# Attention with a parallel MLP on one core: weighted sums in bursts of three key tiles, two in three steps

## The chip, the core and the metric

The kernel runs on one core of a Trainium2 chip. The metric is the time of one execution on the device in microseconds (us); the time of a kernel is the median of its runs. The engines have short names: PE (TensorE) multiplies matrices, PEld is its loading of stationary weights, DVE (VectorE), ACT (ScalarE) and POOL (GpSimd) work element by element, and SP only issues DMAs. Each engine carries out its own instructions in the order in which the kernel issues them, and waits where an operand is not ready or a buffer is not free. Results of PE land in PSUM, eight banks of 128 partitions by 512 f32 numbers; DVE and ACT read them from there.

## The reference

x has 2048 tokens of 448 numbers. One layer norm feeds two branches, and their sum is added to x:

```python
x = A_x
xn = _layernorm(x, axis=-1)
return x + _A_ref(xn, A_wq, A_wk, A_wv, A_wo) + _B_ref(xn, B_w1, B_b1, B_w2, B_b2)
```

Branch A is attention with 16 query heads of width 28 that share one head of keys and one of values:

```python
scores = jnp.einsum("bhqd,bkd->bhqk", q, k) * (Dh ** -0.5)
p = _softmax(scores, axis=-1)
o = jnp.einsum("bhqk,bkd->bhqd", p, v)
return (lambda x, *d: x.transpose(*d))(o, 0, 2, 1, 3).reshape(B, S, H * Dh) @ wo
```

Branch B normalizes once more, goes up to 1792 numbers with a GELU, and back to 448.

## The kernel before

The work has two phases. The first one (up to about 480 us) computes q, k, v and the MLP. The second one is the loop over `steps` at lines 871 to 912, and only this loop and what it calls is touched.

Queries are cut into 4 chunks of 512 and heads into 4 groups of 4, which gives 16 units (c, g); unit u is `units[u]`. Keys are cut into 16 key tiles of 128. A step is two key tiles of one unit, so a unit is 8 steps and the loop has 128 steps, numbered n from 0. The softmax needs the largest score of each query first, so scores are computed twice: once with queries on the partitions for the maximum, and once with keys on the partitions for the exponentials.

In units 1 to 15 (`TURNED`) the last of the four heads goes another way. Its scores are computed once, with queries on the partitions; the maximum and the exponential are taken there; the result goes to DRAM (`td`), and comes back in blocks (`half`) that DVE transposes. The three other heads, and all four of unit 0, are scored twice.

What a step does, and in which order, is a string of letters in `ORDERS`. There is one set of strings for unit 0 and one for the others, and the strings of a set are taken in turn by the number of the step. The letters are:

- `s`: one score tile of 128 keys by 512 queries (`score`, line 852). PE writes one PSUM bank (line 860), ACT takes the exponential of it into half of a weight buffer `p` (line 861).
- `m`: one tile for the maximum (`max_stream`, line 507). PE writes a bank (517), DVE reduces it (518). Its quota follows `weight` (line 875): an `m` is left out where the stream is ahead.
- `t`: one tile of the turned head (`turned_scores`, 545). PE writes a bank (551), DVE copies it with its maximum into one of two `raw` buffers (552). Four of them fill a `raw` buffer.
- `x`: half of the exponential of a full `raw` (`turned_exp`, 564; ACT, line 569). After the second half SP stores `raw` in four DMAs (572). A `raw` buffer can be written again when its store has read it.
- `T`: DVE transposes the turned head's blocks of this step's two key tiles (`turn_blocks`, 841) into one weight buffer.
- `P`: a burst of weighted sums, `BURST` key tiles long (`pv`, 824). For each key tile four heads run side by side in four strips of 32 columns of PE, two instructions each, so a burst of two key tiles is 16 instructions (line 829). They add into `po`, the eighth bank.
- `n`, `o`: one piece of the normalization of the unit before (`norm_jobs`, 754), and of the output projection (`o_jobs`, 734). `e`: the transposed maxima of the next unit, at one step of each unit (`load_max`, 493).

At the start of a step `load_d` (706) has DVE write one number into a `half` buffer and SP load into it (line 712 is that memset). A `half` buffer is a quarter-by-quarter filled block of eight key tiles, and there are three.

Tiles for `s`, `m`, `t`, `e` and `o` share a ring of seven PSUM banks (line 700):

```python
mp = ctx.enter_context(tc.tile_pool(name="ring", bufs=7, space=PSUM))
```

PE can start such a tile only when one of these banks has been read. The weight buffers `p` hold two tiles of 128 by 512, and there are `PAIRS` of them; a step of a turned unit takes four. `P` at step n reads the key tiles in order, behind the scores, and its buffers are free again after it. The last 11 steps (`LEAD`) have no `m`.

Of the kernel before, what the change touches and what calls it, by code (L numbers as in the profile page):

```python
# [8 lines left out]
F32 = mybir.dt.float32  # L9
F32R = mybir.dt.float32r  # L10
# [5 lines left out]
P = 128  # L16
S, D, H, DH, F = 2048, 448, 16, 28, 1792
NT = S // P
CT = 4
NCH = NT // CT  # L20
CW = CT * P
NG = H // 4
NF = F // P
EPS = 1e-5
SCALE = DH ** -0.5
BURST = 2
PAIRS = 9
MLP_MAX = 18
ORDERS = (("nsmsmsnomssmstmssxmP", "nsmsmsemssmsomssnxmP"), ("nmsstTmsosnmssP", "nmsmssxmeosTmsnsmP"))
TURNED = tuple(range(1, 16))  # L30
RAWS = 2
GELU = 0.044715, 0.7978845608028654
LEAD = 11
# [5 lines left out]
def block_kernel(ctx, tc, x, wq, wk, wv, wo, w1, b1, w2, b2, out):  # L39
# [4 lines left out]
    def f(t):  # L44
        return t.bitcast(F32)
# [8 lines left out]
    def heads_of(u):  # L54
        return 3 if u in TURNED else 4
# [56 lines left out]
    def mtile(shape):  # L112
        return mp.tile(shape, F32, name="m")
# [97 lines left out]
    def bn_end(c, k0=0, n=CT):  # L211
        for k in range(k0, k0 + n):
            dve.bn_aggr(lnp[:, CT * c + k, :], sts[c][:, k, :])
        ts = slice(CT * c + k0, CT * c + k0 + n)
        r = rstd(lnr[:, ts], lnp[:, ts, 1], n)
        next(r)
        yield
        next(r)
        dve.scalar_tensor_tensor(lnb[:, ts], lnp[:, ts, 0], -1.0, lnr[:, ts], op0=ALU.mult, op1=ALU.mult)
        yield  # L220
# [9 lines left out]
    def norm_both():  # L230
        dve.tensor_mul(lnq, lnp[:, :, 1], lnr)
        dve.tensor_mul(lnq, lnq, lnr)
        r = rstd(lnq, lnq, NT)
        next(r)
        yield
        next(r)
        dve.tensor_mul(lnq, lnq, lnr)
        dve.scalar_tensor_tensor(lnqb, lnp[:, :, 0], -1.0, lnq, op0=ALU.mult, op1=ALU.mult)
        act.activation(warm, one, AF.Tanh)
        yield  # L240
# [61 lines left out]
    def norm_gen(c, bank):  # L302
        center, turn = norm_parts(c, True, False, bank)
        for k in range(CT + 1):
            if k > 0:
                turn(k - 1)
            yield
            if k < CT:
                center(k)
            yield  # L310
# [83 lines left out]
    def spin(n, t=None):  # L394
        for _ in range(n):
            pe.matmul(idle if t is None else t, ident, ident, start=True, stop=True)
# [9 lines left out]
    for c, at in ((2, ((0, 1), (0, 2), (0, 2), (0, 3))), (3, ((1, 0), (1, 1), (1, 2), (1, 3)))):  # L406
        for k in range(CT):
            later(*at[k], lambda t=CT * c + k: bn(t))
        g = bn_end(c)
        for k in range(2):  # L410
            later(c - 1, 0, lambda g=g: next(g), True)
    g = norm_both()
# [13 lines left out]
    qss, ots = {}, {}  # L426
# [15 lines left out]
    for c in range(NCH):  # L442
        center, turn = norm_parts((c + 1) % NCH, c + 1 == NCH)
        for i in range(4):
# [7 lines left out]
            if i in ((2, 3) if c == 0 else (1, 3)):  # L452
                n = 2 * c + i // 3
# [209 lines left out]
    for c in range(1, NCH):  # L663
        g = norm_gen(c, lambda shape: php.tile(shape, F32, name="ph"))
# [4 lines left out]
    for n in range(len(mslots) + 2):  # L669
        c, ft = mslots[n] if n < len(mslots) else (NCH, n - len(mslots))  # L670
# [28 lines left out]
    att = ctx.enter_context(tc.tile_pool(name="att", bufs=2))  # L699
    mp = ctx.enter_context(tc.tile_pool(name="ring", bufs=7, space=PSUM))  # L700
    op = ctx.enter_context(tc.tile_pool(name="op", bufs=1, space=PSUM))

    wor = att.tile([P, NG, D], F32, name="wor", bufs=1)
    halves = {}

    def load_d(u, i):
# [5 lines left out]
        dve.memset(part[0:1, 0, 0:1], 0.0)  # L712
        nc.sync.dma_start(part, td[u][:, r, :, 256 * h:256 * h + 256])

    woh = att.tile([P, NG, D], F32R, name="woh", bufs=1)
    wol = att.tile([P, NG, D], F32R, name="wol", bufs=1)
    pool.memset(wor, 0.0)
# [10 lines left out]
    def load_rows_of(c, tiles):  # L728
        for k in tiles:
            rows[c, k] = keep.tile([P, D], F32, name="a", bufs=4)  # L730
            dve.memset(rows[c, k][0:1, 0:1], 0.0)
            nc.sync.dma_start(rows[c, k], ad[:, CT * c + k, :])

    def o_jobs(c, gs, tiles=range(CT)):
        last = NG - 1 in gs
        for k in tiles:
            po = mtile([P, D])
            ts = slice(k * P, (k + 1) * P)
            for g in gs:
                oth, otl = ots[c, g]  # L740
                pe.matmul(po, oth[:, ts], woh[:, g, :], start=(g == gs[0]), stop=False)  # L741
                pe.matmul(po, oth[:, ts], wol[:, g, :], start=False, stop=False)  # L742
                pe.matmul(po, otl[:, ts], woh[:, g, :], start=False, stop=(g == gs[-1]))  # L743
            a = rows[c, k]
            dve.tensor_add(a, a, po)
            if last:
                (nc.scalar if k % 2 and c == NCH - 1 else nc.sync).dma_start(ov[:, CT * c + k, :], a)
            yield

    def o_tiles(c, g):  # L750
        ots[c, g] = [att.tile([P, CW], F32R, name=n, bufs=5) for n in ("oth", "otl")]
        return ots[c, g]

    def norm_jobs(u, po):
# [36 lines left out]
    def end_jobs(u, po):  # L791
        while side.step() or oside.step():
            pass
        c, g = units[u]
        oth, otl = o_tiles(c, g)
        jobs = o_jobs(c, [g])
        tr, rb, on = att.tile([P, CW], F32, name="tr2", bufs=1), att.tile([P, CW], F32, name="tr", bufs=1), att.tile([P, CW], F32, name="oc", bufs=1)
        rc = att.tile([P, CW // 32], F32, name="rc", bufs=1)
        last = mtile([P, P])
        spin(9, last)  # L800

        def blocks(t, h):
            return t[:, h].rearrange("p (a b) -> p a b", b=32)

        def shares(i):
            h, r = slice(256 * i, 256 * i + 256), slice(8 * i, 8 * i + 8)
            dve.transpose(tr[:, h], po[:, h])
            dve.reciprocal(rc[:, r], blocks(tr, h)[:, :, 0])
            dve.transpose(blocks(rb, h), rc[:, r, None].to_broadcast([P, 8, 32]))
            dve.tensor_mul(on[:, h], po[:, h], rb[:, h])  # L810
            act.activation(oth[:, h], on[:, h], AF.Copy)
            return lambda: dve.tensor_sub(otl[:, h], on[:, h], f(oth[:, h]))

        low = shares(0)
        low()
        low = shares(1)
        next(jobs)
        low()
        for _ in jobs:
            pass  # L820
# [3 lines left out]
    def pv(u, kt):  # L824
        if kt == 0:
            pos[u] = op.tile([P, CW], F32, name="po")
        po = pos[u]
        for j in range(4):
            pe.matmul(po[32 * j:32 * j + 32, :], vs[:, kt, :], ps.pop((u, kt, j)),  # L829
                      start=(kt == 0), stop=(kt == NT - 1))  # L830
        if kt == NT - 1:
            if u == NU - 1:
                end_jobs(u, pos.pop(u))
                return
            side.add(norm_jobs(u, pos.pop(u)))
            side.step()
            c, g = units[u]
            if c < NCH - 1 and g == NG - 1:
                oside.add(o_wait(c, range(NG), range(CT)))
# [7 lines left out]
    def pair_of():  # L847
        return att.tile([P, 2, CW], F32, name="p", bufs=PAIRS)

# [14 lines left out]
    def o_wait(c, gs, tiles):  # L864
        for k in range(4):
            load_rows_of(c, tiles[k:k + 1])
            yield
            yield
        yield from o_jobs(c, gs, tiles)

    steps = [(u, kt) for u in range(NU) for kt in range(0, NT, 2)]
    pvq = [(u, kt) for u in range(NU) for kt in range(NT)]
    total = 4 * CT * len(heads)
    left = total - maxed
    weight = [0 if n >= len(steps) - LEAD else (3, 5)[n % 2] + (u == 0) for n, (u, kt) in enumerate(steps)]
    for n, (u, kt) in enumerate(steps):
        if n == 0:
            loads = pool
        if n == len(steps) - 14:
            load_rows_of(NCH - 1, range(CT))  # L880
        if u + 1 < NU:
            load_d(u + 1, kt // 2)
        if 4 <= n < 4 + NG:
            prep_wo(n - 4)
        if u + 1 < NU and kt < 8:
            load_q(u + 1, (kt // 2,))
        jobs = [(u, kt + k, j) for k in range(2) for j in range(heads_of(u))]
        for what in ORDERS[u in TURNED][n % 2]:
            if what == "s":
                score(*jobs.pop(0))  # L890
            elif what == "m":
                if maxed < total - left + left * sum(weight[:n + 1]) / sum(weight):
                    maxed += mxs.step()
            elif what == "t":
                tq.step()
            elif what == "x":
                turned_exp()
            elif what == "T":
                if u in TURNED:
                    turn_blocks(u, kt)  # L900
            elif what == "e":
                if kt == (6 if u + 2 < NU else 10) and u + 1 < NU:
                    load_max(u + 1)
            elif what == "n":
                side.step()
            elif what == "o":
                if n == len(steps) - 5:
                    oside.add(o_jobs(NCH - 1, range(NG - 1)))
                oside.step()
            elif what == "P":  # L910
                assert not jobs
                for _ in range(BURST if n else 0):
                    pv(*pvq.pop(0))
    while pvq:
        pv(*pvq.pop(0))
    while side.step():
# [26 lines left out]
```

## Time and profile before

| | |
|---|---|
| time, median of 3 runs (lowest, highest) | 1094.62 us (1094.16, 1096.04) |
| profiled execution: time, span | 1097.33 us, 1095.6 us |
| granted TensorE clock in it | 0.996 |
| PE, DVE, ACT, POOL busy, share of the span | 99%, 83%, 67%, 51% |

Steps can be found in the trace by the first score matmul (line 860) of each: step 0 starts at 480.5 us, step 8 (the first of unit 1) at 521.0 us, step 117 (the first without `m`) at 1038.2 us, and the last weighted sum starts at 1084.7 us. A row of the timeline gives start and length in us, the engine, the line, the operation, the tiles (out<-in), the shape and how many instructions were merged into the row; in brackets stands idle time before it and what ended that. A row of the windows gives, for each engine, its busy time in the stretch and the number of its instructions, then the clock, the share of the DMA engines and the rate. A matmul's length in a row covers its whole passage, so rows overlap; from start to start the distance is shorter.

### The profile page before, as it was taken

How to read it: one execution, taken by the hardware profiler on the slowest of the kernel's cores; microseconds unless marked ns; L12 is line 12 of the kernel's file. 1: busy time of each engine (PE TensorE's matmuls, PEld its weight loads, DVE VectorE, ACT ScalarE, POOL GpSimd, SP SyncE). 2: the span in 40 equal slices, each digit the busy share in tenths (PEclk: the TensorE clock that was granted, in tenths of full speed). 3: DMA queues.
4: the chain of work that ended last, by engine and by line, in shares of the span. 5: the costliest groups of instructions: out<-in, count | busy, mean ns of one | idle time of the engine just before them, and what ended most of it. 6: DMA issues, size and time to landing. Idle time of an engine off the chain costs nothing.

```text
span 1095.6 us, 17543 instructions
## 1 busy us (share of the span) xinstructions
PE 1080.2 (99%) x5777; PEld 715.9 (65%) x5777; DVE 909.2 (83%) x1847; ACT 736.7 (67%) x1279; POOL 561.0 (51%) x694
## 2 busy tenths in 40 slices
PE   9989999999999999999999999999999999999998
PEld 8768888888888888865555555555546454555444
DVE  7768899888988998886888997799987898886743
ACT  6765555666666666658777776677775777765783
POOL 6347788768767777764334433433442343343220
PEclk9989999999999999999999999999999999999999
DMA  8675546777877777877977798588796678895720
GB/s 280 206 230 136 137 120 161 196 177 190 209 184 181 192 195 170 216 169 156 204 186 173 182 227 215 129 199 190 181 215 174 174 175 200 199 199 131 182 52 35
DMA packets 140512, 195.15 MB, mean 178 GB/s; under 512 B 17086, under 2 KB 96116, under 8 KB 140420
## 3 DMA queue, kind: packets, MB, share of 16 engines
q1 hardware_dynamic: 127684, 172.11, 62.9%
q0 software_dynamic: 11328, 21.33, 8.7%
q8 instruction: 46, 0.75, 0.3%
q10 hardware_dynamic: 1408, 0.57, 0.2%
q14 instruction: 46, 0.38, 0.1%
HBM read 115.22 MB, written 77.71 MB: 176 GB/s over the span
## 4 chain that ended last, share of the span: by engine, by line
PE 92%; DVE 5%; ACT 1%; issue 1%; DMA 1%; SPq 0%; ACTq 0%; DVEq 0%
PE po L829 22%; PE m L517 18%; PE m L860 17%; PE ph L179 10%; PE m L551 5%; PE m L628 4%; PE m L625 4%; PE m L631 4%; PE m L741 1%; PE ph L182 1%; PE ph L184 1%; PE m L742 1%; PE m L743 1%; DVE mx L518 1%; PE qp L179 1%
## 5 line engine op out<-in xcount | busy, mean ns | idle before, releaser
L518 DVE TENSOR_REDUCE mx<-m 128x1 f32<-128x512 f32 x784 | 506.4, 679 | 80.8 <-PE m L517 71.9
L861 ACT ACTIVATE p<-m 128x512 f32<-128x512 f32 x784 | 402.5, 609 | 163.3 <-PE m L860 163.2
L517 PE MATMUL m<-ks,qm 128*128 128x512 f32 x784 | 322.2, 411 | 0.0
L860 PE MATMUL m<-xh,ks 128*128 128x512 f32 x784 | 258.7, 399 | 0.9 <-DVE half L712 0.9
L829 PE MATMUL po<-p,vs 128*32 128x512 f32 x2048 | 246.0, 598 | 0.0
L517 PEld LDWEIGHTS m<-ks,qm 128*128 128x128 f32 x784 | 147.0, 187 | 117.3 <-ACT p L861 35.4
L860 PEld LDWEIGHTS m<-xh,ks 128*128 128x128 f32 x784 | 144.4, 188 | 51.0 <-ACT p L861 13.6
L552 DVE TENSOR_SCALAR_CACHE_REDUCE raw<-m 128x512 f32<-128x512 f32 x240 | 161.0, 689 | 18.9 <-PE m L551 10.8
L843 DVE STREAM_TRANSPOSE p<-half 128x1024 f32<-128x1024 f32 x120 | 148.2, 1236 | 5.3 <-PE po L829 3.3
L569 ACT ACTIVATE raw<-raw,m 128x1024 f32<-128x1024 f32 x120 | 133.1, 1151 | 0.0
L829 PEld LDWEIGHTS po<-p,vs 128*32 128x32 f32 x2048 | 53.5, 109 | 120.2 <-issue 114.2
L599 ACT ACTIVATE hx<-ph,b1t 128x512 f32<-128x512 f32 x56 | 38.6, 690 | 135.3 <-PE ph L184 128.8
L551 PE MATMUL m<-ks,q 128*128 128x512 f32 x240 | 95.7, 399 | 0.6 <-DVE mx L518 0.6
L614 POOL TENSOR_TENSOR hl<-hx,hh 128x512 fp32r<-128x512 f32 x56 | 72.9, 1302 | 35.3 <-ACT hh L612 35.3
L631 PE MATMUL m<-w2h,hl 128*128 128x448 f32 x224 | 82.8, 369 | 0.3 <-POOL hl L614 0.3
L628 PE MATMUL m<-w2l,hh 128*128 128x448 f32 x224 | 81.6, 364 | 0.0
L625 PE MATMUL m<-w2h,hh 128*128 128x448 f32 x224 | 81.5, 364 | 0.0
L504 POOL DMA_DIRECT2D xh<-mn x15 | 8.1, 543 | 131.5 <-ACT mn L500 131.5
L607 POOL TENSOR_TENSOR hx<-hx,hz 128x512 f32<-128x512 f32 x56 | 72.9, 1302 | 4.7
L602 POOL TENSOR_TENSOR hz<-hz,hx 128x512 f32<-128x512 f32 x56 | 72.6, 1296 | 4.7
L179 PE MATMUL ph<-xh,w1h 128*128 128x512 f32 x168 | 67.2, 400 | 4.6 <-ACT hz L600 4.6
L179 PE MATMUL ph<-xh,w1l 128*128 128x512 f32 x168 | 66.4, 395 | 0.0
(167 smaller groups left out, 1369.5 us busy)
## 6 DMA issues: line engine op xcount, KB each, us to landing
td<-raw SPq DMA_DIRECT2D x240, 256.0 KB
half<-td SPq DMA_DIRECT2D x120, 512.0 KB
xh<-qd POOLq DMA_DIRECT2D x60, 168.0 KB, 4.2
a<-in_A_x_dram SPq DMA_DIRECT2D x32, 224.0 KB
qm<-qd POOLq DMA_DIRECT2D x112, 56.0 KB, 4.4
qd<-qe SPq DMA_DIRECT2D x24, 256.0 KB
qm<-qd SPq DMA_DIRECT2D x84, 56.0 KB
ad<-a SPq DMA_DIRECT2D x16, 224.0 KB
```

The costliest lines, as they stand in the source:

```text
L179: pe.matmul(ps, w, v, start=(n == 0), stop=False)
L517: pe.matmul(pm, qm[:, t * P:(t + 1) * P], ks[:, n * CW:(n + 1) * CW], start=True, stop=True)
L518: dve.tensor_reduce(mx[:, CT * j + t, n:n + 1], pm, axis=AX.X, op=ALU.max)
L551: pe.matmul(sc, q3[i][:, t * P:(t + 1) * P], ks[:, n * CW:(n + 1) * CW], start=True, stop=True)
L552: dve.tensor_scalar(raw[:, :, 4 * n:4 * n + 4, :].rearrange("p r b i -> p b r i"), sc.rearrange("p (b r i) -> p b r i", r=4, i=32), SCALE, ...
L569: act.activation(raw[:, rs], raw[:, rs], AF.Exp, bias=m3[:, 4:5], scale=1.0)
L628: pe.matmul(m2[k], hh[:, ts], w2l[:, ft, :], start=False, stop=False)
L631: pe.matmul(m2[k], hl[:, ts], w2h[:, ft, :], start=False, stop=(ft == NF - 1))
L829: pe.matmul(po[32 * j:32 * j + 32, :], vs[:, kt, :], ps.pop((u, kt, j)), start=(kt == 0), stop=(kt == NT - 1))
L843: dve.transpose(p.rearrange("p k (g j) -> p g k j", j=32), halves[u, kt // 8][:, :, 32 * (kt % 8):32 * (kt % 8) + 64].rearrange("p g (k j) ...
L860: pe.matmul(s, ks[:, kt * P:(kt + 1) * P], qss[u][:, j, :], start=True, stop=True)
L861: act.activation(p, s, AF.Exp, scale=SCALE)
```

## The change

`BURST` goes from 2 to 3 key tiles and each set of `ORDERS` from two strings to three. Two of the three strings have a `P`, so three steps (six key tiles) have two bursts of three. In the turned set the bursts stand at the end of the first string and in the middle of the third; each string has four `m`, where before one had three and the other five. `t` stands twice in each string of unit 0 (before once in two steps) and once in three steps later (before once in two). `x` stands once in each step of unit 0, as before, and once in three steps later (before once in two). `T` moves to the end of its string, or two letters ahead of a `P` that ends it.

Weight buffers go from 9 to 12. To find room for them, `wor` (the raw output weights) no longer has a buffer of its own: it takes the first of the three `half` buffers; `oth` and `otl` have four buffers each in place of five; and the end of the kernel transposes into a weight buffer instead of `tr2`. The quota weight is 4 in every step (5 in unit 0) instead of 3 and 5 in turn (4 and 6). The assertion that all scores of a step were issued moves to the end of the step, since `P` no longer always ends it.

```diff
-BURST = 2
-PAIRS = 9
+BURST = 3
+PAIRS = 12
 MLP_MAX = 18
-ORDERS = (("nsmsmsnomssmstmssxmP", "nsmsmsemssmsomssnxmP"), ("nmsstTmsosnmssP", "nmsmssxmeosTmsnsmP"))
+ORDERS = (("nsmsmstemssmsomsxnsmtP", "nsmsmstemssmsomsxnsmt", "nsmsmstmsPxmsmsonsmst"),
+          ("nmsmessomsmnsTsP", "nsmsmssmosmnesT", "nmssmxtsPmsmoesnsT"))
...
-    wor = att.tile([P, NG, D], F32, name="wor", bufs=1)
...
+    half = att.tile([P, 4 * CT, 256], F32, name="half", bufs=3)
+    wor = half.rearrange("p g c -> p (g c)")[:, 0:NG * D].rearrange("p (g n) -> p g n", g=NG)
...
-        ots[c, g] = [att.tile([P, CW], F32R, name=n, bufs=5) for n in ("oth", "otl")]
+        ots[c, g] = [att.tile([P, CW], F32R, name=n, bufs=4) for n in ("oth", "otl")]
...
-        tr, rb, on = att.tile([P, CW], F32, name="tr2", bufs=1), att.tile([P, CW], F32, name="tr", bufs=1), att.tile([P, CW], F32, name="oc", bufs=1)
+        tr, rb, on = pair_of()[:, 0], att.tile([P, CW], F32, name="tr", bufs=1), att.tile([P, CW], F32, name="oc", bufs=1)
...
-    weight = [0 if n >= len(steps) - LEAD else (3, 5)[n % 2] + (u == 0) for n, (u, kt) in enumerate(steps)]
+    weight = [0 if n >= len(steps) - LEAD else 4 + (u == 0) for n, (u, kt) in enumerate(steps)]
...
-        for what in ORDERS[u in TURNED][n % 2]:
+        for what in ORDERS[u in TURNED][n % 3]:
...
             elif what == "P":
-                assert not jobs
                 for _ in range(BURST if n else 0):
                     pv(*pvq.pop(0))
+        assert not jobs
```

## The prediction

> **What bounds the kernel now.** First the page, for the busy shares and the chain that ended last; then the windows, cut at the steps named above; then the timeline around single bursts.
>
> ```profile
> span 1095.6 us, 17543 instructions
> ...
> PE 1080.2 (99%) x5777; PEld 715.9 (65%) x5777; DVE 909.2 (83%) x1847; ACT 736.7 (67%) x1279; POOL 561.0 (51%) x694
> ...
> PE 92%; DVE 5%; ACT 1%; issue 1%; DMA 1%; SPq 0%; ACTq 0%; DVEq 0%
> ```
>
> ```profile
> core 0: us, PE busy (x) PEld busy (x) DVE busy (x) ACT busy (x) POOL busy (x), PEclk, DMA share, GB/s
> 0.00:480.50 480.50, 470.16 (x2203) 393.55 (x2203) 415.15 (x942) 299.76 (x434) 345.67 (x351) 0.99 0.70 185
> 480.50:521.00 40.50, 40.50 (x223) 22.38 (x223) 28.21 (x59) 35.63 (x71) 19.25 (x29) 1.00 0.82 180
> 521.00:1038.20 517.20, 517.20 (x3029) 272.54 (x3027) 442.25 (x811) 365.61 (x704) 188.25 (x307) 1.00 0.80 186
> 1038.20:1084.70 46.50, 46.50 (x299) 23.41 (x295) 17.55 (x21) 34.89 (x69) 7.82 (x10) 1.00 0.20 41
> ```
>
> PE carries 92% of the chain. In steps 8 to 116 (521 to 1038 us) it never rests, DVE is busy 442 of 517 us and ACT 366. So a PE cycle saved there is time saved, but DVE has only 14% to spare: wherever an order bunches DVE's work, the next bound is near. A busy PE can still lose time between instructions; the timeline shows where.
>
> ```profile
> 699.45 1.92 PE L829 MATMUL po<-p,vs 128*32 128x512 f32 x16
> 701.30 0.50 PE L517 MATMUL m<-ks,qm 128*128 128x512 f32 x1
> 701.64 0.63 PE L860 MATMUL m<-xh,ks 128*128 128x512 f32 x2
> 702.11 0.39 PE L551 MATMUL m<-ks,q 128*128 128x512 f32 x1
> 702.33 0.40 PE L517 MATMUL m<-ks,qm 128*128 128x512 f32 x1
> 702.57 0.62 PE L860 MATMUL m<-xh,ks 128*128 128x512 f32 x2
> 703.02 0.39 PE L517 MATMUL m<-ks,qm 128*128 128x512 f32 x1
> 703.25 0.61 PE L860 MATMUL m<-xh,ks 128*128 128x512 f32 x2
> 703.79 1.93 PE L829 MATMUL po<-p,vs 128*32 128x512 f32 x16
> 705.65 0.50 PE L517 MATMUL m<-ks,qm 128*128 128x512 f32 x1
> ...
> 1081.62 3.64 PE L829 MATMUL po<-p,vs 128*32 128x512 f32 x32
> ```
>
> This is one step. From 701.64 to 703.25 lie seven intervals between tiles: 1.61/7 = 0.23 us a tile. The last burst of the kernel has 16 instructions more than the others and takes 3.64 - 1.92 = 1.72 us more: 0.86 us a key tile with no edge. The step, 699.45 to 703.79, takes 4.34 us and holds 10 tiles and one burst: 4.34 - 10 x 0.23 - 1.72 = 0.32 us belong to the burst's two edges (the tile after it follows after 0.34 us in place of 0.23, and so on). That is what a longer burst saves.
>
> **Part 1: fewer bursts, -13.4 us.** Before, steps 1 to 127 have one each: 127. After, strings one and three of each set have one: steps 3, 6, ..., 126 and 2, 5, ..., 125, 84 bursts, and one more for the last four key tiles: 85. 42 x 0.32 = 13.4 us, all on PE's path. The Trainium skill (TensorEngine Tiling (Array Packing), section Key Properties) says that changing the tiling mode drains TensorE; the edges of the 128*32 bursts agree, at the 0.32 us above, and by that rule alone nothing but the gain would be left.
>
> **Part 2: a stall in the stretch between the middle burst and the next, +19.2 us.** In a turned period of three steps the tiles are cut by two bursts into two stretches: 16 tiles with one `T` between them, and 15 tiles `m s m s s [T] m s m s s m s m s [T] s`. The rows for a walk through the second:
>
> ```profile
> L518 DVE TENSOR_REDUCE mx<-m 128x1 f32<-128x512 f32 x784 | 506.4, 679 | 80.8 <-PE m L517 71.9
> L861 ACT ACTIVATE p<-m 128x512 f32<-128x512 f32 x784 | 402.5, 609 | 163.3 <-PE m L860 163.2
> L843 DVE STREAM_TRANSPOSE p<-half 128x1024 f32<-128x1024 f32 x120 | 148.2, 1236 | 5.3 <-PE po L829 3.3
> L569 ACT ACTIVATE raw<-raw,m 128x1024 f32<-128x1024 f32 x120 | 133.1, 1151 | 0.0
> ```
>
> ```profile
> 702.07 3.04 ACT L861 ACTIVATE p<-m 128x512 f32<-128x512 f32 x6 [1.38 <-PE m L860]
> 703.34 1.23 DVE L843 STREAM_TRANSPOSE p<-half 128x1024 f32<-128x1024 f32 x1
> 704.50 1.25 DVE L518 TENSOR_REDUCE mx<-m 128x1 f32<-128x512 f32 x2
> 705.81 0.06 DVE L712 MEMSET half<- 1x1 f32 x1
> 706.19 1.29 DVE L518 TENSOR_REDUCE mx<-m 128x1 f32<-128x512 f32 x2 [0.32 <-PE m L517]
> ```
>
> ```profile
> 543.86 2.56 ACT L861 ACTIVATE p<-m 128x512 f32<-128x512 f32 x5 [1.31 <-PE m L860]
> 544.51 0.19 PEld L860 LDWEIGHTS m<-xh,ks 128*128 128x128 f32 x1 [0.19 <-ACT p L861]
> 544.59 0.41 PE L860 MATMUL m<-xh,ks 128*128 128x512 f32 x1
> ```
>
> Exponentials follow each other after (3.04 - 0.61)/5 = 0.49 us, reductions after 0.60 (1.25 or 1.29 for two, less 0.68), and a reduction starts 1.16 after a `T`, or 1.35 where the memset of a step's start comes between (1.23, 0.06 pause, 0.06). A reader starts 0.43 after its tile (701.64 to 702.07), 0.54 after the first of a stretch (705.65 to 706.19). A waiting tile starts 0.12 after the reader that frees its bank (543.86 + 0.61 to 544.59).
>
> Now the walk; zero is the stretch's first tile. Tile k starts at 0.34 + 0.23(k - 1). ACT frees the banks of the `s` tiles 1, 3, 4, 6, 8, 9 at 1.38, 1.87, 2.35, 2.84, 3.32, 3.81. DVE frees tiles 0 and 2 at 1.22 and 1.82, then does the `T` from 1.74, then the memset, and frees tiles 5, 7, 10 at 3.77, 4.37, 4.97. Tiles 7 to 11 find banks. Tile 12, due at 2.87, needs the sixth free bank (2.84 + 0.12): 0.09 late. Tile 13, due at 3.19, needs the one of 3.32: 0.25 late. Tile 14, due at 3.67, needs the one of 3.77: 0.22 late. Together 0.56 us, in which PE stands with all seven banks full. The same walk through the first stretch finds a bank ready for each of its 16 tiles, because its `T` comes after ten. Before, the stretches have 10 and 11 tiles, and the rows above show starts every 0.23 us without a break.
>
> 0.56 holds if each tile gets the bank that is free first. Were the seven given in strict turn, tile 12 would wait for tile 5 (3.77 + 0.12 - 2.87 = 1.02) and tile 14 for tile 7 (0.14): 1.16 us. The rows at 543.86 speak against strict turn: the tile at 544.59 waits for an exponential that began 0.73 us before it, and whose own tile began 0.43 us earlier, five tiles back (1.16/0.23) and not seven. So I take 0.60, near the lower value. There are 36 such stretches (steps 8 to 116); in about 4 of them pieces of the output projection give DVE time. 32 x 0.60 = 19.2 us, on PE's path; ends 0 (readers faster than the rows) and 37. The Trainium skill (TensorEngine Tiling (Array Packing), section PSUM Bottleneck) warns that tiling speeds up TensorE but not PSUM evacuation; the walk agrees, but no row before shows it as lost PE time.
>
> **Part 3: `t` twice a step in unit 0, +6.5 us.** The number of `t` stays 48, so PE and DVE do no more; but a `raw` buffer now fills in two steps, not eight, and the next but one needs its store read out.
>
> ```profile
> DVE raw L552 <- DMA td<-raw: 2.5, 3, 1.4
> ```
>
> ```profile
> td<-raw SPq DMA_DIRECT2D x240, 256.0 KB
> half<-td SPq DMA_DIRECT2D x120, 512.0 KB
> ```
>
> A store is four DMAs, 1.05 MB; at the 180 GB/s of 480.5:521.0 that is 5.8 us (DMA is 82% busy there, and SP has a 512 KB load a step ahead of it). With the exponential (1.15, behind two others) and the issue it lands about 8.3 us after its `x` is reached. Three times a `t` wants that buffer: in step 4, 5.0 us after the `x` of step 3 (three tiles, a burst, six tiles) and 0.4 of DVE's own lag: DVE waits 2.9; in step 6, 7.2 us after the `x` of step 5: 1.1; in step 8 only 3.1 us after that of step 7 (eight tiles, no burst): 5.2. That is 9.2 us of DVE; behind the waiting `t` stand all later reductions, and PE goes on until the seven banks are full, about 0.9 us each time: 9.2 - 2.7 = 6.5. Ends: 0 (the three such waits in the first phase were short) and 15 (a store half as fast).
>
> **Parts at nothing.** `wor` in a `half` buffer: four readers at steps 4 to 7, next load at step 8; if they were late, DVE's memset would wait. `oth`, `otl` four: a new one is wanted 14.5 steps after a chunk's last unit, its last reader is done after 13; without that cover POOL waits, not PE. Twelve weight buffers: four a step, so each is taken again three steps later, after its burst. End transposing into a weight buffer: its burst is long over. The moved `T` and `x`: weights are needed a step later; SP's loads follow the memset as before. Last `t` at step 101, last store at step 107, load at step 112. The even quota moves reductions between neighbours only. In the last 11 steps no `m` is left, so the gain of part 1 stands.
>
> **Sum.** 1097.3 (profiled execution) - 13.4 + 19.2 + 6.5 = 1109.6. The median of the runs is 2.7 below the profiled execution: 1107.
>
> **Rivals.**
> - A, the forecast: 1107; with parts 2 and 3 at 0.4 to 0.8 us and 2 to 10 us, 1096 to 1117. Chance 0.45.
> - B, banks in nearly strict turn, so that PE waits for the reductions behind `T` each period: 1094.6 - 13.4 + 37 + 6.5 = 1125. Against it the early bank at 544.59. Chance 0.12.
> - C, stores land late, since DMA is already 82% busy in unit 0: part 3 at 15, 1115. Chance 0.15.
> - D, the other side: the stall behind `T` doesn't occur because the readers catch up during the longer bursts (2.57 us), and then the stores have their time as well: 1094.6 - 13.4 = 1081. DVE's 14% of idle time speaks for it, the seven banks against it. It decides from the point where the stall falls below (13.4 - 6.5)/32 = 0.22 us a period. Chance 0.20. By the skill's draining rule alone the time would be this one.
> - E, gain and losses cancel: 0.08.
>
> A measurement of this kernel tells about 0.2% from no change, 1092.4 to 1096.8. Slower: A + B + C = 0.72; same 0.08; faster 0.20. The range 1084 to 1124 leaves out most of D and the upper part of B, about 0.2.
>
> **What would show it.** Right: 85 bursts, 84 of them with 24 instructions, with tiles every 0.23 us in the first stretch of a period; in the second, three tiles late, by half a microsecond together, waiting for ACT's `p` and DVE's `mx`, so that three steps take 0.56 - 0.32 = 0.24 us more than before; at steps 4, 6 and 8 DVE's line 552 waits for DMA `td<-raw`, longest at step 8, and PE stands there. Wrong: starts every 0.23 us throughout (D), or a single wait of a microsecond behind each `T` (B), or waits on `half` or `p` that I put at nothing.

## The result, and the profile after

The changed kernel takes 1134.41 us (median of 5 runs, 1132.32 to 1136.3), the one before on the same chip 1094.16 (1093.3 to 1096.04): a ratio of 1.036, interval 1.0343 to 1.0377. It is slower, as forecast, but by 40 us in place of 12. The profiled execution took 1136.3 us, with a span of 1134.5. The page of the changed kernel, busy shares and chain:

```profile
span 1134.5 us, 17512 instructions
...
PE 1102.8 (97%) x5777; PEld 721.1 (64%) x5777; DVE 911.9 (80%) x1847; ACT 734.7 (65%) x1279; POOL 561.8 (50%) x694
...
PE 86%; DVE 4%; ACT 3%; DMA 3%; issue 2%; SPq 0%; POOL 0%; POOLq 0%; ACTq 0%; DVEq 0%
```

No engine has more work than before: the number of PE instructions is the same, 5777, and DVE's time has grown by 3 us. PE now rests, and is busy 97% of the span and not 99%; its share of the chain falls from 92% to 86%. The time is lost to waits. Most of it does not show as rest: the rows of two tiles overlap, so a tile that starts a little late only lengthens the busy time, which grows from 1080.2 to 1102.8 us for the same instructions. Of the 38.9 us that the span gains, only 16.3 are rest of PE. The windows from step 0 on, cut at the same events as before (first score of step 0, of step 8, of step 117, last weighted sum):

```profile
core 0: us, PE busy (x) PEld busy (x) DVE busy (x) ACT busy (x) POOL busy (x), PEclk, DMA share, GB/s
479.20:532.80 53.60, 49.55 (x218) 24.57 (x219) 36.07 (x83) 39.91 (x74) 17.79 (x26) 0.94 0.73 171
532.80:1073.70 540.90, 530.46 (x3025) 275.10 (x3025) 434.94 (x785) 358.09 (x699) 188.80 (x308) 1.00 0.73 174
1073.70:1123.30 49.60, 46.88 (x304) 23.96 (x303) 19.27 (x25) 36.02 (x72) 8.76 (x11) 1.00 0.20 43
```

Unit 0 is 13.1 us longer than before, steps 8 to 116 are 23.7 longer, the last steps 3.1. In unit 0 the mean granted clock is 0.94.

The starts of PE's instructions, put beside their usual distances (0.2325 us for a tile, 0.34 after a burst, 0.43 for four side-by-side weighted sums), give what each kind of delay takes. From the same count over the trace of before:

| where | late tiles and burst edges, before | after | waits inside a burst, before | after |
|---|---|---|---|---|
| unit 0 | 0.7 | 12.9 | 0 | 0 |
| steps 8 to 116 | 2.4 | 29.8 | 0 | 9.7 |
| steps 117 to 127 | 0 | 2.6 | 0 | 0 |

The difference is 51.9 us; less the 13.4 that were forecast for the fewer bursts it is 38.5, and the spans differ by 1134.5 - 1095.6 = 38.9. So PE's own delays hold the whole loss. They are of four kinds, and each has its rows.

**First: the stall that was forecast.** PE's timeline in the second stretch of a period. The first of these rows is the eighth tile of 15:

```profile
735.04 0.39 PE L518 MATMUL m<-ks,qm 128*128 128x512 f32 x1
735.26 0.61 PE L862 MATMUL m<-xh,ks 128*128 128x512 f32 x2
735.74 0.50 PE L518 MATMUL m<-ks,qm 128*128 128x512 f32 x1
736.08 0.40 PE L862 MATMUL m<-xh,ks 128*128 128x512 f32 x1
736.32 0.41 PE L518 MATMUL m<-ks,qm 128*128 128x512 f32 x1
736.72 0.98 PE L862 MATMUL m<-xh,ks 128*128 128x512 f32 x2
737.63 1.06 PE L831 MATMUL po<-p,vs 128*32 128x512 f32 x8
```

and the weight loads of the last two tiles, from PEld's timeline:

```profile
736.72 0.19 PEld L862 LDWEIGHTS m<-xh,ks 128*128 128x128 f32 x1 [0.30 <-ACT p L863]
737.21 0.19 PEld L862 LDWEIGHTS m<-xh,ks 128*128 128x128 f32 x1 [0.30 <-ACT p L863]
```

Up to 735.74 a tile starts every 0.23 to 0.24 us. Then three tiles come late, by 0.34 - 0.23 = 0.11, by 0.40 - 0.23 = 0.17 and by 0.49 - 0.23 = 0.26: 0.54 us together, where the walk had 0.56 (for tiles 12, 13 and 14; here they are 11, 13 and 14, counted from 0).

**Second: a wait inside a burst, at the end of a unit.** PE's timeline, and after it ACT's:

```profile
580.67 1.47 PE L831 MATMUL po<-p,vs 128*32 128x512 f32 x12
582.90 1.07 PE L831 MATMUL po<-p,vs 128*32 128x512 f32 x8 [0.77 <-ACT oc L759]
```

```profile
582.25 0.60 ACT L759 ACTIVATE oc<-po 128x512 f32<-128x512 f32 x1 [0.85 <-issue]
```

All weighted sums of a unit add into the one bank `po`. When the unit's 16 key tiles are in, ACT copies the bank to `oc`; only then can the next unit's first key tile be added. Before, a unit ended with a burst, and PE computed ten tiles during the copy. Now a unit's end falls inside a burst of three at 10 of its 15 places (16 is not a multiple of 3), and PE stands in the middle of the burst. PE's wait, with total, number and longest:

```profile
PE po L831 <- ACT oc L759: 8.1, 10, 1.0
```

The view counts PE's rest alone, 8.1 us. From start to start, against the usual 0.43, it is 0.97 us each time, the 9.7 of the table.

**Third: the stores of `raw`.** The waits, then DVE's and PE's timelines:

```profile
DVE raw L553 <- ACT p L863: 11.8, 2, 6.0
```

```profile
501.59 1.29 DVE L519 TENSOR_REDUCE mx<-m 128x1 f32<-128x512 f32 x2 [1.89 <-PE m L518]
508.71 0.69 DVE L553 TENSOR_SCALAR_CACHE_REDUCE raw<-m 128x512 f32<-128x512 f32 x1 [5.84 <-ACT p L863]
...
541.22 0.69 DVE L553 TENSOR_SCALAR_CACHE_REDUCE raw<-m 128x512 f32<-128x512 f32 x1 [5.97 <-ACT p L863]
```

DVE stands 5.84 us in step 4 and 5.97 us in step 8, at the copy into `raw`. (Step 8 is the first of unit 1, so the second of these waits lies in the stretch of steps 8 to 116.) The page of the profile names ACT; the instruction waits for several semaphores, and an experiment below shows that it is the store of the buffer. While DVE stands, PE fills its seven banks and slows down, and then something follows that the forecast does not have (windows of 4 us):

```profile
504.00:508.00 4.00, 2.53 (x6) 0.93 (x5) 0.00 (x0) 3.50 (x7) 1.26 (x2) 1.00 0.92 237
508.00:512.00 4.00, 3.31 (x10) 1.62 (x13) 3.20 (x9) 1.27 (x3) 0.23 (x1) 0.50 0.13 31
512.00:516.00 4.00, 4.00 (x24) 0.73 (x19) 2.46 (x5) 1.56 (x2) 0.00 (x0) 0.64 0.77 198
516.00:520.00 4.00, 3.81 (x19) 2.81 (x16) 3.22 (x8) 3.15 (x7) 0.55 (x1) 1.00 0.78 201
```

DVE is busy 0.00 us in the first row. In the second, when DVE works again, the granted clock is 0.50, and the burst that starts then takes longer than the same burst elsewhere:

```profile
511.82 4.26 PE L831 MATMUL po<-p,vs 128*32 128x512 f32 x24
...
559.96 2.78 PE L831 MATMUL po<-p,vs 128*32 128x512 f32 x24
```

The same follows the wait in step 8: there the clock is 0.50 for 3.41 us.

```profile
542.16:545.57 3.41, 3.41 (x10) 1.65 (x13) 3.33 (x6) 1.91 (x4) 0.00 (x0) 0.50 0.16 35
```

**Fourth: one wait near the end.** A score of the last unit waits for its maxima, whose DMA POOL issues behind a transfer of the normalization; the waits, then POOL's timeline:

```profile
PE m L862 <- DMA xh<-mn: 2.3, 1, 2.3
```

```profile
1076.36 2.02 POOL L779 DMA_DIRECT2D tr<-ld  x4 [4.77 <-DMA ld<-rc]
1078.37 0.52 POOL L505 DMA_DIRECT2D xh<-mn  x1
```

POOL waits 4.77 us for the DMA `ld`, and the maxima stand behind it.

### The profile page after: what moved, and what is told of

It is laid out like the page before. It is cut to its first block, busy times and chain, and to the rows that moved or that the text cites. A ratio compares the mean times of both kernels' runs of the same rounds, so it can differ in the third digit from the quotient of the medians.

```text
span 1134.5 us, 17512 instructions
## 1 busy us (share of the span) xinstructions
PE 1102.8 (97%) x5777; PEld 721.1 (64%) x5777; DVE 911.9 (80%) x1847; ACT 734.7 (65%) x1279; POOL 561.8 (50%) x694
## 4 chain that ended last, share of the span: by engine, by line
PE 86%; DVE 4%; ACT 3%; DMA 3%; issue 2%; SPq 0%; POOL 0%; POOLq 0%; ACTq 0%; DVEq 0%
PE po L831 19%; PE m L862 17%; PE m L518 16%; PE ph L180 10%; PE m L552 5%; PE m L629 4%; PE m L626 4%; PE m L632 4%; ACT p L863 1%; DVE mx L519 1%; PE ph L185 1%; PE ph L183 1%; PE m L745 1%; PE m L743 1%; PE m L744 1%
## 5 line engine op out<-in xcount | busy, mean ns | idle before, releaser
L862 PE MATMUL m<-xh,ks 128*128 128x512 f32 x784 | 289.9, 416 | 6.3 <-DMA xh<-mn 2.3
L831 PE MATMUL po<-p,vs 128*32 128x512 f32 x2048 | 241.0, 600 | 8.1 <-ACT oc L759 8.1
L553 DVE TENSOR_SCALAR_CACHE_REDUCE raw<-m 128x512 f32<-128x512 f32 x240 | 160.8, 687 | 30.1 <-ACT p L863 11.8
L831 PEld LDWEIGHTS po<-p,vs 128*32 128x32 f32 x2048 | 57.2, 110 | 141.3 <-issue 121.8
L487 POOL DMA_DIRECT2D xh<-qd x60 | 38.4, 640 | 60.3 <-PE m L518 43.4
```

The lines of the kernel that those rows point to most:

```text
L553: dve.tensor_scalar(raw[:, :, 4 * n:4 * n + 4, :].rearrange("p r b i -> p b r i"), sc.rearrange("p (b r i) -> p b r i", r=4, i=32), SCALE, ...
L862: pe.matmul(s, ks[:, kt * P:(kt + 1) * P], qss[u][:, j, :], start=True, stop=True)
```

## The experiments

Ratios are against the kernel before; "after" is the changed kernel, 1134.41 us. None of these kernels leaves out any of the computation. The lengths of unit 0, of steps 8 to 116 and of the last steps are cut at the same events as above.

| kernel | us | ratio (interval) | unit 0 | steps 8 to 116 | last steps |
|---|---|---|---|---|---|
| before | 1094.16 | | 40.5 | 517.2 | 46.5 |
| after | 1134.41 | 1.036 (1.0343, 1.0377) | 53.6 | 540.9 | 49.6 |
| e1_stop | 1121.61 | 1.0233 (1.0218, 1.0249) | 53.3 | 529.1 | 47.6 |
| e6_split (from before) | 1131.4 | 1.0328 (1.0308, 1.0349) | 41.8 | 550.2 | 48.1 |
| e4_te | 1129.51 | 1.0303 (1.0282, 1.0323) | 54.1 | 536.6 | 47.4 |
| e7_plan | 1127.0 | 1.0289 (1.0266, 1.0312) | 49.2 | 536.8 | 49.1 |
| e8_plan_te | 1113.7 | 1.0177 (1.0158, 1.0197) | 49.2 | 526.1 | 47.0 |
| e2_x | 1134.1 | 1.0349 (1.0331, 1.0366) | 57.0 | 537.7 | 47.7 |
| e5_all | 1121.38 | 1.023 (1.0209, 1.0251) | 57.6 | 525.6 | 47.4 |
| e9_u0 | 1123.93 | 1.0265 (1.0244, 1.0285) | 40.4 | 543.4 | 48.3 |
| e12_raw3 | 1124.43 | 1.0274 (1.026, 1.0288) | 47.6 | 537.7 | 50.8 |
| e10_best | 1099.92 | 1.0041 (1.0028, 1.0055) | 40.5 | 518.1 | 51.0 |
| e13_two | 1090.59 | 0.9954 (0.9941, 0.9966) | 43.9 | 507.9 | 47.0 |
| e14_three | 1091.49 | 0.996 (0.9947, 0.9974) | 43.6 | 510.3 | 47.8 |

### Bursts that stop at a unit's end (e1_stop)

Where a unit would end inside a burst, the burst ends with the unit, two or four key tiles long. The number of bursts stays.

```diff
-                for _ in range(BURST if n else 0):
-                    pv(*pvq.pop(0))
+                goal = 2 * n + (-1 if n % 3 == 2 else 0) if n else 0
+                for end in (goal - 1, goal + 1):
+                    if end % NT == 0 and 0 < end < len(steps) * 2:
+                        goal = end
+                while NU * NT - len(pvq) < goal:
+                    pv(*pvq.pop(0))
```

> Bursts end at a unit's last key tile (2 or 4 key tiles there, same number of bursts), so no burst needs the po bank twice. Theory (each wait adds to PE's chain by itself): the ten waits of PE for ACT's copy of po, 0.97 us each in the changed kernel's trace, go: 9.7 us less, about 1124.7. Rival (DVE and ACT are the bound over a period, so a wait taken from PE comes back as a fuller ring): less than 4 us gained, 1130 or more, with more time in late tiles.

Measured: 12.8 us less than after. No wait of `po` for `oc` inside a burst is left, and steps 8 to 116 are 11.8 shorter, 9.7 of them these waits. Another 2.0 come from the last steps. The middle stretch:

```profile
532.20:1061.30 529.10, 527.97 (x3025) 274.52 (x3025) 434.72 (x785) 357.62 (x699) 189.17 (x308) 1.00 0.75 178
```

PE is busy 528 of 529 us. So the bank `po` costs some 10 to 12 us. The late tiles, counted without the starts of the bursts, are hardly touched (24.8 us; after: 26.0).

### What a burst's two edges cost (e6_split)

The kernel before, with each burst cut in two and tiles between the halves: the same instructions, and 127 bursts more.

```diff
-BURST = 2
+BURST = 1
-ORDERS = (("nsmsmsnomssmstmssxmP", "nsmsmsemssmsomssnxmP"), ("nmsstTmsosnmssP", "nmsmssxmeosTmsnsmP"))
+ORDERS = (("nsmsmsnomssmstmssxPmP", "nsmsmsemssmsomssnxPmP"), ("nmsstTmsosnmsPsP", "nmsmssxmeosTmsnsPmP"))
```

> The kernel before with each burst of two key tiles split into two of one, a tile between them. Theory (0.32 us for the two edges of a burst, worked out of one step): 127 more bursts, 41 us more, 1135. Rival (the edges are cheaper, and the changed kernel lost its gain there): 15 us more or less, 1110.

Measured (2 runs): 35.6 us more than before (1095.79 on that chip): 35.6/127 = 0.28 us a burst, 0.27 to 0.30 by the interval. The price of the first part, 0.32, was near; 42 bursts less are worth 11.8 us.

### `T` earlier in the stretch (e4_te)

In the third turned string `T` goes ahead of the burst, out of the stretch of 15 tiles; the order of all else stays.

```diff
-          ("nmsmessomsmnsTsP", "nsmsmssmosmnesT", "nmssmxtsPmsmoesnsT"))
+          ("nmsmessomsmnsTsP", "nsmsmssmosmnesT", "nmssmxtsTPmsmoesns"))
```

> The T of the third turned string is put just ahead of that string's P, so that DVE transposes during the burst and not in the 15 tiles after it. Theory (the ring of seven fills behind that T): the late tiles of the first string's steps (22.5 us together) fall to 3 or so, about 1114. Rival (DVE has too little idle time wherever T stands): the late tiles only move to the other stretch, 1128 or more.

A miss: 4.9 us less than after, 2.2 of it in the last steps. The late tiles in steps 8 to 116 went from 26.0 to 23.3 us only. So taking the `T` out does not end the stall by itself, though the walk had given its length.

### The banks chosen by reckoning (e7_plan), and with `T` earlier (e8_plan_te)

The walk takes it that each tile gets the bank that is free first. The bank of each tile is fixed when the program is built, by the framework and not by the chip. The trace shows whether it was the first one free: each tile is put beside its reader, and the tiles not yet read are counted at the moment when a late tile was due. Where there are fewer than seven, a bank was free, and the tile waited for another. In steps 8 to 116 such waits come to 2 us before, 11 after and 23 in e4_te. So here the kernel names the bank itself: a small reckoning with rows of the trace (PE 0.23 us a tile, ACT 0.48, DVE 0.60, `T` 1.16) is carried along while the program is written out, and picks the bank that is free first by it. Nothing else is changed.

```diff
     def mtile(shape, kind="o"):
-        return mp.tile(shape, F32, name="m")
+        b = min(range(7), key=lambda i: free[i])
+        at = max(ring["pe"], free[b] + 0.12)
...
+        start = max(ring[eng], seen + (2.2 if kind == "o" else 0))
+        ring[eng], free[b] = start + step, start + took
+        return mp.tile(shape, F32, name=f"m{b}", bufs=1)
```

> The changed kernel with the ring's banks given by a small reckoning in the kernel (PE 0.23 us a tile, ACT 0.48, DVE 0.60, T 1.16; the bank that is free first by it) in place of the build's own choice. Theory (the late tiles are a matter of seven banks and of the readers, the choice adds a third): of some 30 us of late tiles in steps 8 to 116 about 10 go, 1124. Rival (the choice is as good as can be): within 3 us of the changed kernel, 1131 to 1137.

> The same reckoning with T ahead of the middle burst. Theory (moving T does what the walk said, and the build's choice of banks hid it): late tiles of steps 8 to 116 fall from 25 to 5 us, 1109. Rival (ACT and DVE are too slow for 15 tiles between bursts whatever the bank): 1123 or more.

Measured: the banks alone give 7.4 us (by the profiled executions 4.1 in steps 8 to 116 and 4.4 in unit 0). With `T` earlier as well it is 20.7 us less than after, and 15.8 less than e4_te: of the steps 8 to 116, 540.9 us after, there are left

```profile
532.00:1068.60 536.60, 525.50 (x3025) 271.37 (x3025) 433.50 (x786) 358.24 (x699) 189.01 (x308) 1.00 0.75 176
```

with `T` earlier alone, and

```profile
527.40:1053.50 526.10, 513.20 (x3026) 275.90 (x3025) 433.53 (x788) 357.65 (x700) 188.91 (x309) 0.99 0.78 179
```

with both. The same stretch of the period, from the timeline of e8_plan_te (PE's lines are L535 for `m`, L886 for `s`, L854 for weighted sums there):

```profile
727.21 0.50 PE L535 MATMUL m<-ks,qm 128*128 128x512 f32 x1
727.55 0.65 PE L886 MATMUL m<-xh,ks 128*128 128x512 f32 x2
728.13 1.07 PE L854 MATMUL po<-p,vs 128*32 128x512 f32 x8
```

The two last scores need 0.58 us from their start to that of the burst; after the change they needed 0.91. The count of unread tiles tells why the two edits need each other. For steps 18 to 116, well behind the wait in step 8, the late tiles take (us, rounded):

| kernel | all seven banks unread | a bank was free | together |
|---|---|---|---|
| after | 14.1 | 7.0 | 21.2 |
| e4_te, `T` earlier | 0.2 | 17.7 | 18.0 |
| e7_plan, banks by reckoning | 13.8 | 2.0 | 15.8 |
| e8_plan_te, both | 1.2 | 5.2 | 6.4 |

With `T` in the stretch all seven banks are full whichever is chosen; with `T` out of it a bank is free, but the program has named another. The forecast of 1109 us was missed by 4.7: of the 14.5 us of late tiles left in steps 8 to 116, where 5 were expected, 8.1 lie in steps 8 to 17, in and behind the wait in step 8, which neither edit touches.

### `x` earlier in unit 0 (e2_x), and all three cures (e5_all)

The exponentials in unit 0 are put early in the step, so that the stores start sooner. e5_all has this, the stop at a unit's end, and the earlier `T`.

```diff
-ORDERS = (("nsmsmstemssmsomsxnsmtP", "nsmsmstemssmsomsxnsmt", "nsmsmstmsPxmsmsonsmst"),
+ORDERS = (("nsmxsmstemssxmsomsnsmtP", "nsmxsmstemssmsomsxnsmt", "nsmsmstmsPxmsmsonsmst"),
```

> Unit 0 only: a second x in each string, so that both halves of a full raw buffer are exponentiated in one step and its store leaves a step earlier; nothing else moves. Theory (DVE waits for the store's read of raw at steps 4 and 8, 5.8 and 6.0 us): both waits go, unit 0 falls from 53.6 to about 43 us, 1124. Rival (unit 0 is long because 24 tiles without a burst fill the ring): the stretch stays at 50 us or more, 1131 or more.

> The three edits together. Theory (three separate waits, each on PE's chain): 1134.4 - 9.7 - 10 - 20 = about 1095, level with the kernel before or a little faster. Rival (they share one cause, DVE's load): the sum falls short by 10 us or more, 1105 or more.

Two misses. With `x` early, DVE's long waits are gone, and unit 0 is still 57.0 us long, 3.4 more than after: two exponentials of 1.15 us now stand in one step of ACT, ahead of the scores' exponentials, so that the banks of the scores are freed later. That this is the cause is not shown; in 12.9 of the 14.0 us of late tiles in unit 0 another bank was free. And the clock still falls:

```profile
508.00:512.00 4.00, 3.57 (x13) 1.67 (x17) 2.00 (x4) 1.57 (x3) 0.00 (x0) 0.50 0.89 247
```

All three together gain what the stop alone gains (1121.38 against 1121.61): unit 0 loses what the earlier `T` brings.

### Unit 0 as before (e9_u0)

Unit 0 keeps its two old strings and bursts of two; the `t` and `x` that it then lacks go into the turned strings.

```diff
+ORDERS = (("nsmsmsnomssmstmssxmP", "nsmsmsemssmsomssnxmP"),
+          ("nmsmxessomsmnsTsP", "nsmsmssmosmtnesT", "nmssmxtsPmsmoesnsT"))
...
-        for what in ORDERS[u in TURNED][n % 3]:
+        for what in ORDERS[u in TURNED][n % (3 if u else 2)]:
```

> Unit 0 as in the kernel before (its two strings, bursts of two), the turned strings with a second t in three steps and a second x; all else as changed. Theory (unit 0's new strings fill the ring and wait for the raw store, and the clock drops behind it): unit 0 back from 53.6 to 41 us, and the later steps longer by 0 to 5 us, 1122 to 1127. Rival (the start of the loop is slow from DMA load, by the half buffer of the output weights): unit 0 at 48 us or more, 1130 or more.

Measured: 10.5 us less than after. Unit 0 is as short as before the change, and the clock stays at 1.00:

```profile
477.40:517.80 40.40, 40.38 (x222) 22.46 (x223) 28.10 (x59) 35.59 (x71) 19.00 (x28) 1.00 0.80 179
```

Steps 8 to 116 are 2.5 longer than after, since the `t` have moved there. All of unit 0's loss belongs to its new strings.

### A third `raw` buffer (e12_raw3)

The changed kernel, with every third `raw` in a buffer of its own, so that no `t` wants a buffer whose store is still being read.

```diff
-            raw = keep.tile([P, 4, NT, 32], F32, name="raw", bufs=RAWS)
+            third = late.get("n", 0) % 3 == 2
...
+            raw = (late["pool"] if third else keep).tile([P, 4, NT, 32], F32, name="raw", bufs=1 if third else RAWS)
```

> The changed kernel with a third raw buffer in the loop (8 KB more), so that no t waits for a store; ACT's and PE's order as in the changed kernel. Theory (unit 0 loses 13 us to the two waits for the store and to the half clock that follows them): unit 0 from 53.6 to about 44 us, 1125. Rival (ACT and the ring are the limit in 24 tiles without a burst): unit 0 at 50 us or more, 1131 or more.

Measured: 10.0 us less than after, as expected, but spread otherwise: unit 0 is 47.6 us long, 6.0 less (3.6 longer than expected), and steps 8 to 116 are 3.2 shorter, since the wait in step 8 lay there. The two waits of 5.8 and 6.0 us at the copy into `raw` are gone, and with them the two falls of the clock behind them; all that line has left of waits for a store is

```profile
DVE raw L556 <- DMA td<-raw: 0.8, 2, 0.6
```

So the waits that the page of the profile put down to ACT were waits for the store. 7.3 us of late tiles remain in unit 0 without them. It is not that up to 24 tiles without a burst are too many for seven banks: in 6.4 of the 7.3 us a bank was free. PE's and ACT's timelines there:

```profile
517.99 0.50 PE L867 MATMUL m<-xh,ks 128*128 128x512 f32 x1
518.33 0.40 PE L518 MATMUL m<-ks,qm 128*128 128x512 f32 x1
519.18 0.50 PE L867 MATMUL m<-xh,ks 128*128 128x512 f32 x1 [0.45 <-ACT p L868]
```

```profile
518.53 0.60 ACT L868 ACTIVATE p<-m 128x512 f32<-128x512 f32 x1 [1.26 <-PE m L867]
```

The tile at 519.18 starts when ACT has read the one of 517.99. Only these two tiles are unread then; five other banks stand empty. e14_three below has the same strings in unit 0 and the banks by reckoning, and its unit 0 takes 43.6 us.

### All cures together (e10_best, e13_two, e14_three)

e10_best: unit 0 as before, stop at a unit's end, earlier `T`, banks by reckoning.

> All four cures together: bursts that stop at a unit's end, T of the third string ahead of its burst, banks by the reckoning, unit 0 as in the kernel before. Theory (four separate losses on PE's chain over a gain of about 12 us): 1134.4 - 12.8 (stops) - 20.7 (T and banks) - 10.5 (unit 0) = 1090.4, some 4 us under the kernel before. Rival (the cures overlap, or the second t in three steps fills the ring again): 1097 or more.

A miss by 9.5 us. The last steps take 51.0 us in place of 46.5, through the wait that the changed kernel has too; POOL's and PE's timelines:

```profile
1042.08 2.02 POOL L800 DMA_DIRECT2D tr<-ld  x4 [4.48 <-DMA ld<-rc]
1044.09 0.52 POOL L522 DMA_DIRECT2D xh<-mn  x1
```

```profile
1052.03 1.64 PE L886 MATMUL m<-xh,ks 128*128 128x512 f32 x6 [2.13 <-DMA xh<-mn]
1053.60 4.40 PE L854 MATMUL po<-p,vs 128*32 128x512 f32 x24
```

After a pause of 2.13 us, 24 instructions take 4.40 us, not the 2.78 of the row at 559.96; the clock is 0.50 there:

```profile
1053.50:1056.92 3.42, 3.42 (x17) 0.80 (x20) 0.00 (x0) 2.08 (x5) 0.00 (x0) 0.50 0.00 0
```

And the second `t` in three steps, which the old unit 0 leaves for later and which ends at step 75, goes with late tiles and bursts of 14.8 us in steps 9 to 75, against 2.2 in steps 76 to 116.

e13_two therefore has bursts of two in unit 0 with two `t` a step, the third `raw`, and the last unit's maxima issued by SP in place of POOL, beside the stop, the earlier `T` and the reckoned banks. e14_three is the same with the changed kernel's own three strings in unit 0.

```diff
-ORDERS = (("nsmsmstemssmsomsxnsmtP", "nsmsmstemssmsomsxnsmt", "nsmsmstmsPxmsmsonsmst"),
+ORDERS = (("nsmsmstnomssmsmssxtmP", "nsmsmstemssmsomssxntmP"),
...
-        loads.dma_start(f(qs[60:61, 0:nh, :]), f(mn[:, 0, :]))
+        q = nc.sync if u == NU - 1 else loads
+        q.dma_start(f(qs[60:61, 0:nh, :]), f(mn[:, 0, :]))
```

> Bursts of three in units 1 to 15 that stop at a unit's end, T of the third string ahead of its burst, banks by the reckoning, third raw buffer; in unit 0 bursts of two in every step with two t, so that the later strings keep one t in three steps; and the last unit's maxima are loaded by SP, not behind POOL's waits. Theory (the late tiles that were left came from the second t, and step 120 waited for POOL's queue): steps 8 to 116 about 507 us, unit 0 about 44, no wait at step 120: 1091. Rival (the tiles of the long stretches stay late): 1097 or more.

> The same cures, with the changed kernel's own strings for unit 0 (bursts of three there too, 24 tiles without a burst). Theory (with a third raw buffer and the reckoning unit 0 loses no more than a few us): unit 0 about 45 us, 1092. Rival (24 tiles without a burst are too many for seven banks): unit 0 at 47 us or more, 1094 or more, slower than the other of this pair.

Both came out as expected: e13_two at 1090.59 us (5 runs, 1090.16 to 1091.35; before 1095.47 on that chip), below both kernels: against the one before by 0.34% to 0.59%, a small difference, but one that the interval keeps clear of zero; e14_three at 1091.49 (1091.2 to 1093.12), 0.26% to 0.53% below it. The windows of e13_two:

```profile
479.10:523.00 43.90, 43.90 (x234) 24.59 (x235) 35.77 (x86) 40.86 (x75) 19.32 (x29) 1.00 0.95 212
523.00:1030.90 507.90, 507.79 (x3009) 275.50 (x3009) 431.57 (x782) 355.70 (x697) 187.17 (x305) 1.00 0.82 185
1030.90:1077.90 47.00, 46.59 (x300) 24.03 (x302) 18.00 (x24) 35.90 (x72) 7.78 (x9) 1.00 0.20 42
```

PE no longer rests, and steps 8 to 116 are 9.3 us shorter than before the change, about 2.8 of them (12 x 0.23) because twelve `t` now lie in unit 0. 8.8 us of late tiles and late bursts are still in them (before: 2.4), which is part of what the fewer bursts should save and don't. e14_three keeps the changed kernel's own unit 0 and bursts of three all through: with the bank `po`, the `raw` stores, `T` and the choice of banks, and POOL's queue seen to, the changed kernel's loss of 40 us is gone.

## Why the prediction was right or wrong

The terms of the sum beside what was measured:

| term | forecast | measured | from |
|---|---|---|---|
| part 1, fewer bursts | -13.4 | -11.8 | e6_split, 42 x 0.28 |
| part 2, stall in the second stretch | +19.2 | +22.5 | late starts in the steps of the first string |
| stalls in the other strings | 0 | +4.9 | 29.8 - 22.5, less 2.4 of before |
| part 3, unit 0 | +6.5 | +12.2 | late starts, 12.9 - 0.7 |
| bank `po` at a unit's end | not named | +9.7 | waits inside bursts; e1_stop gains 12.8 |
| last steps, POOL's queue | 0 | +2.6 | the wait for `xh<-mn` and the late starts by it |

They sum to 40.1; the spans differ by 38.9. The forecast's terms sum to 12.3. Of the 27.8 us between, 9.7 are the bank `po`, 5.7 unit 0, 4.9 the other strings, 3.3 the second stretch, 2.6 the last steps and 1.6 the bursts.

- **Part 1 held.** Its mechanism and its place are right, the size is 0.28 a burst and not 0.32.
- **Part 2 held in place and mechanism, and its size is partly luck.** Three tiles at the end of the second stretch were late by 0.54 us against 0.56, and over the 36 stretches it makes 22.5 against 19.2 (0.62 and 0.60 a stretch, where the forecast took 32 of them). But the walk has all of it with seven full banks, and in steps 18 to 116 only 14.1 of 21.2 us of late tiles are of that kind. The step that fails is "0.56 holds if each tile gets the bank that is free first". The row at 544.59 in the prediction speaks against strict turn, as it says, but it also speaks against this: the tile is the seventh of its stretch, and the readers of the stretch before had ended by 543.0 (DVE's reductions at 541.75, 1.25 us long, and ACT's exponentials at 541.45, 1.10 us long), so that a bank was free while its weight load waited for an exponential. "Finds a bank ready for each of its 16 tiles" fails for the same reason; that and the wait in step 8 are the late tiles in the other strings.
- **Part 3 held in the place of the waits, and its size fell short.** Waits were foretold in steps 4, 6 and 8 with 2.9, 1.1 and 5.2 us; they came in steps 4 and 8, with 5.8 and 6.0. The stores did not land by the 8.3 us from `x`: from the start of the `x` at 498.44 to DVE's restart at 508.71 it is 10.3 us, 9.1 of them from the issue of the store at 499.60. Without these waits e12_raw3 is 10.0 us faster, where the forecast had 6.5. The step that fails is the sum "9.2 - 2.7 = 6.5", which takes the waits too short and charges PE only with the time DVE stands: the fall of the clock behind the pause is left out (its own share was not measured). And unit 0 without these waits is still 7.1 us longer than before (47.6 against 40.5), for which the forecast has no term: the late tiles in its long stretches, most of them with a bank free.
- **"Parts at nothing" failed, and the bank `po` is its largest miss.** It walked through the buffers for weights, outputs and loads, but not through the bank `po` that the weighted sums themselves use: a unit now ends inside a burst at 10 of 15 places, and PE stands 0.97 us each time, 9.7 us, none of it in the sum. The sentence on the last 11 steps, that the gain stands because no `m` is left, took no account of POOL's queue. What was put at nothing on the weight buffers held: DVE waits 2.7 us in all for a free one at its `T`, before 3.3.
- **The rivals.** B falls: no single wait of 1.16 us stands behind `T`. C came nearest in its place: the stores do land late, and their waits, with the clock behind them, cost 10.0 us, between the forecast's 6.5 and C's 15. D falls for this kernel: the readers do not catch up. E falls.

The range reached to 1124 because every bound came from a row that the walk had looked at; `po` was not looked at, and the choice of banks and the clock were in no bound; together they exceed what was left.

## What to carry to other kernels

When a group of work becomes longer, ask of every buffer that it passes through whether its length still divides the buffer's own period: 16 key tiles in bursts of three put ten copies of a single accumulator on the path. Moving an instruction away from a stall and choosing buffers well can each look weak alone (here 4.9 and 7.4 us) and work together (20.7), so test the pair before either is dropped. A tile that waits is no proof that all buffers are full: count the unread ones first. A pause of the bounding engine can cost more than its own length, by what its clock does afterwards.

## What the runs showed of the hardware

The granted clock fell to 0.50 in the 4 us after a stretch in which PE was busy 2.53 of 4 us, and was 0.64 on the mean in the next 4; a burst of 24 instructions then took 4.26 us in place of 2.78. The Trainium skill (TensorE: Matmul & The Clock Gate, Part 1: The HAM clock gate) says that the clock drops to half after about one idle window of 3.4 us. The half agrees; here no pause of PE in that stretch was longer than 1.01 us by the timeline,

```profile
506.60 0.49 PE L518 MATMUL m<-ks,qm 128*128 128x512 f32 x1 [1.01 <-ACT p L863]
507.55 0.49 PE L862 MATMUL m<-xh,ks 128*128 128x512 f32 x1 [0.46 <-ACT p L863]
...
508.73 0.80 PE L518 MATMUL m<-ks,qm 128*128 128x512 f32 x1 [0.69 <-ACT p L863]
```

so several short pauses were enough in this run: the first tile after them takes 0.80 us, not 0.49. In the 3.41 us before the fall PE was busy 1.94 us, and the half clock lasted 6.83 us:

```profile
504.61:508.02 3.41, 1.94 (x4) 0.72 (x4) 0.00 (x0) 2.89 (x5) 0.93 (x1) 1.00 0.96 242
508.02:514.85 6.83, 6.14 (x22) 2.23 (x25) 5.66 (x13) 2.83 (x4) 0.20 (x1) 0.50 0.35 90
```

Which share of busy time it needs to keep its clock was not tried.

A wait for several semaphores was put down to ACT in both of DVE's long waits, at 5.84 and 5.97 us; the third buffer shows that it was the store.
